# Second experts' first products: 15 block products of thirds for 18, and one plan that orders all engines from there on

## The chip, the cores and the metric

The kernel runs on one core of one Trainium2 chip. The metric is the device time of one execution in microseconds (us); lower is better. TensorE (PE) multiplies, ScalarE (ACT) and VectorE (DVE) read the product banks (PSUM) and work on tiles in SBUF, GpSimd (POOL) works on SBUF tiles, and SyncE (SP) issues the loads and stores.

## What is computed

Attention over 1152 tokens, then a feed-forward layer, then eight experts. Only the experts change here:

```python
def _moe2_ref(x, w_gate, w1, w2):          # x 1152x512, w1 8x512x1024, w2 8x1024x512
    P = np.exp(x @ w_gate - (x @ w_gate).max())
    for _ in range(8):
        P /= P.sum(1, keepdims=True) + 1e-09
        P /= P.sum(0, keepdims=True) + 1e-09
        P *= N / E
    for e in range(E):
        out += P[:, e:e + 1] * (np.maximum(x @ w1[e], 0.0) @ w2[e])
```

Every product is made with operands split in a high and a low part (`hi` is the rounded copy, `lo` the rest), as three matmuls: hi by hi, hi by lo, lo by hi. So one block product over 256 of the 512 input features is 2 x 3 = 6 matmuls.

## The kernel before

**Up to the crossing.** Attention and the start of the feed-forward layer come from a planner (`Plan`, with the table `COST` of busy time and latency by kind of step) that fixes the order of every engine. The end of the feed-forward layer (`gemm1`, `gemm2`, lines 456 and 475) follows in loops. Its result x is formed in four groups of 288 tokens.

**First products of the experts.** The 8 x 1024 hidden features are 64 chunks of 128. Two chunks, two halves of the features of x and two halves of the tokens make a 2 x 2 x 2 problem, which the list `PROD` solves with 7 block products in place of 8 (Winograd's form of Strassen's scheme), a quarter of the tokens (288 columns) at a time. `hidden(h, gp)` (matmuls on line 1192) does this for four chunks h and one of two column positions; two pairs of chunks (`u`) alternate, so that product m of both pairs runs before product m+1 of either. The sums of weights are made by DVE (`e_sums`, line 1077) and split by ACT and POOL (`e_block`, lines 1083 and 1084); the sums of tokens are made once, at the crossing. Partial results are copied out of a bank by ACT (`keep`, line 1179), added by DVE, and rectified and split by ACT and DVE (`done`, lines 1183 and 1184).

**Second products.** `outputs(h, j)` multiplies 128 tokens by the rows of four chunks, 12 matmuls of 512 columns in one bank (line 1230), and DVE adds the bank to `yacc`, with the gate's factor P (line 1241). The rows of w2 are split by ACT and POOL (lines 1104 and 1105). The gate's logits are 40 matmuls of 288 columns (line 1121).

**The crossing** from the feed-forward layer to the experts is written by hand: `first_sums`, `second_sums` and `crossing` (lines 1267 to 1400) interleave the last sums of the feed-forward layer (`inner`, line 1267), the sums of tokens (lines 1275 to 1302) and the first seven products (`product`, line 1315). After it, the tile framework's scheduler chooses the order.

Of the kernel before, what the change touches and what calls it, by code (L numbers as in the profile page):

```python
# [49 lines left out]
    "sum": ("ACT", 0.295, 0.45), "load": ("SP", 0.45, 0.0),  # L50
}
# [10 lines left out]
PORT = {"shift", "sign", "tail", "m", "g", "scale", "fscale", "guard", "vsum", "vsum2", "clamp", "glo", "wlo"}  # L62
# [38 lines left out]
class Step:  # L101
    def __init__(self, **kw):
        self.__dict__.update(kw)
        self.after, self.before, self.left, self.done, self.tail, self.t = [], [], 0, None, 0.0, 0.0


class Plan:
# [34 lines left out]
    def lay(self, tails):  # L142

        rings = {id(z.ring): z.ring for x in self.steps for z in x.b}.values()
        for ring in rings:
            ring.own, ring.k = [None] * len(ring.own), 0
            for z in ring.all:
                z.spot = None
        for x in self.steps:
            x.left, x.done, x.t = len(x.before), None, 0.0  # L150
# [6 lines left out]
        while ready:  # L157
# [20 lines left out]
            if x.eng == "PE" and gap > 0.3:  # L178
# [18 lines left out]
            for y in x.after:  # L197
                y.left -= 1
                y.t = max(y.t, x.done + SEM)
                if not y.left:  # L200
                    ready.append(y)
        if len(log) < len(self.steps):
            return None
        return log

    def back(self, log):
# [3 lines left out]
        behind, ahead, owner = {id(x): list(x.after) for x in self.steps}, {id(x): list(x.before) for x in self.steps}, {}  # L210
# [34 lines left out]
    def run(self):  # L245
# [5 lines left out]
        for n in range(ROUNDS):  # L251
            log = self.lay(tails)
            if not log:
                break
            found.append((self.worth(log), n, log))
            tails = [y + NOISE * rnd.gauss(0.0, 1.0) for y in self.back(log)]
        self.log = min(found)[2]
        for _, x, new, small in self.log:
# [4 lines left out]
            self.emit(x.fn)  # L263
# [3 lines left out]
def attn_moe_moe_kernel(  # L267
# [71 lines left out]
    wg = const.tile([128, KD, NE], F32, name="wg")  # L339

# [27 lines left out]

    def load_w64():
# [13 lines left out]
    def w_raw():  # L383
# [54 lines left out]
    gq, acc, ysum, gl, tx = {}, {}, {}, {}, {}  # L438
# [21 lines left out]
    def gemm2(s):  # L460
# [8 lines left out]
        for d in range(KD):  # L469
# [87 lines left out]
    RE, RMM, RL = (tiles(ap, [128, NMAX], F32, z, 2) for z in ("me", "mm", "ml"))  # L557
# [467 lines left out]
    tx["hi"], tx["lo"] = (tp.tile([128, 3 * KH, NB], F32R, name=f"t{z}") for z in ("hi", "lo"))  # L1025
    for s in range(ATT_END, NS):
# [10 lines left out]
        with tc.issue_after(last["pe"]):  # L1037
# [26 lines left out]

    def e_next(kind, i):
        e_load(order2.index((kind, i)) + ERAW)

    def e_sums(h):

        src = {}  # L1070
        for u in (2 * h, 2 * h + 1):
            r = rw.pop((1, u)).rearrange("p (a b) -> p a b", a=KD)
            s = new(tp, [128, KD * NMAX], F32, "sums", 2)[:, 0:KD * KH * 128].rearrange("p (o a b) -> p o a b", o=4, a=KH)
            w11, w12, w21, w22 = (r[:, k, 128 * f:128 * f + 128] for f in range(2) for k in (first, second))
# [426 lines left out]
```

## Time and profile before

| | |
|---|---|
| runs | 1068.99 us median of 3 (1066.86 to 1069.5) |
| profiled execution, span from first to last instruction | 1065.7 us (the page gives no other time for it) |
| PE busy | 1057.4 us, 99% of the span |
| DVE, ACT, POOL busy | 567.2, 482.8, 338.8 us |
| granted TensorE clock, mean | 0.999 of 2.4 GHz |
| HBM read | 59.93 MB |

A busy time is the union of the times of an engine's instructions. A matmul's row gives its full latency, and the next one starts long before it ends, so a matmul's cost on the path is the distance between starts, not its mean. The rows of DVE, ACT and POOL also overlap a little at their ends.

### The profile page before, as it was taken

Reading aid. Unit: us, or ns where it says so; the run is one execution under the profiler, and the core shown is the slowest. Engines: PE = TensorE matmul, PEld = TensorE weight load, DVE = VectorE, ACT = ScalarE, POOL = GpSimd, SP = SyncE. Lnnn points to the kernel's source line nnn. Section 1 sums busy time; section 2 is a strip of 40 time slices with the busy share of each in tenths; the row PEclk is TensorE's granted clock in tenths of the full one; section 3 lists DMA queues with packets and bytes.
Section 4 is the critical chain, followed back from the end, with each engine's and each line's share of the span. In section 5 each row is a group of like instructions: output and inputs, shape, how many; then the busy total and the mean of one; then the engine's idle time right before and its main releaser. Section 6 shows DMA issues by size and latency. Waiting matters only on the chain.

```text
span 1065.7 us, 19197 instructions
## 1 busy us (share of the span) xinstructions
PE 1057.4 (99%) x7551; PEld 963.6 (90%) x7551; DVE 567.2 (53%) x1225; ACT 482.8 (45%) x1367; POOL 338.8 (32%) x382
## 2 busy tenths in 40 slices
PE   8999999999999999999999999999999999999998
PEld 5899899999998889898898998989999989899997
DVE  6899865452486664545445354444535444444343
ACT  6897875343366434242433424242443424244330
POOL 0343244022047266150513415051432505052300
PEclk9999999999999999999999999999999999999999
DMA  9571322211013020111201111120201111020002
GB/s 220 167 208 38 92 80 79 80 61 40 1 40 99 1 80 31 50 41 40 80 20 60 35 46 40 40 73 9 79 20 60 41 40 47 33 80 21 21 6 84
DMA packets 50179, 63.53 MB, mean 60 GB/s; under 512 B 14888, under 2 KB 33832, under 8 KB 50088
## 3 DMA queue, kind: packets, MB, share of 16 engines
q1 hardware_dynamic: 50088, 62.30, 19.3%
q8 instruction: 59, 0.97, 0.4%
q14 instruction: 32, 0.26, 0.1%
HBM read 59.93 MB, written 2.36 MB: 58 GB/s over the span
## 4 chain that ended last, share of the span: by engine, by line
PE 94%; ACT 2%; DMA 2%; DVE 1%; SPq 1%; issue 0%; POOL 0%; DVEq 0%
PE bank L1230 37%; PE bank L1192 32%; PE bank L456 7%; PE bank L475 7%; PE bank L897 2%; DMA raw<-in_moe_w_in_dram 2%; PE bank L953 2%; PE bank L1315 1%; ACT pl L678 1%; PE bank L611 1%; PE bank L1267 1%; PE bank L738 1%; PE bank L795 1%; PE bank L785 1%; ACT pg L678 1%; PE bank L1121 0%
## 5 line engine op out<-in xcount | busy, mean ns | idle before, releaser
L1230 PE MATMUL bank<-wc,hhi 128*128 128x512 f32 (+1 forms) x1160 | 363.7, 392 | 0.3 <-DVE cs L1154 0.3
L1230 PEld LDWEIGHTS bank<-wc,hhi 128*128 128x128 f32 x1160 | 211.3, 188 | 37.4 <-DVE cs L1154 0.5
L1230 PE MATMUL bank<-wc,hlo 128*128 128x512 f32 x580 | 226.0, 390 | 0.0
L1192 PE MATMUL bank<-xhi,wb 128*128 128x288 f32 x992 | 211.1, 295 | 0.0
L1105 POOL TENSOR_TENSOR wc<-raw,wc 128x512 fp32r<-128x512 f32 x64 | 81.8, 1300 | 341.2 <-ACT wc L1104 341.2
L1192 PEld LDWEIGHTS bank<-xhi,wb 128*128 128x128 f32 x992 | 163.9, 188 | 2.0
L1192 PE MATMUL bank<-thi,wb 128*128 128x288 f32 x744 | 164.6, 295 | 0.0
L1179 ACT ACTIVATE p<-bank 128x288 f32<-128x288 f32 x186 | 76.4, 411 | 173.3 <-PE bank L1192 168.2
L1192 PE MATMUL bank<-xlo,wb 128*128 128x288 f32 x496 | 146.5, 295 | 0.0
L1183 ACT ACTIVATE hhi<-bank 128x288 fp32r<-128x288 f32 x186 | 75.6, 407 | 149.6 <-PE bank L1192 118.3
L1241 DVE SCALAR_TENSOR_TENSOR yacc<-bank,P,yacc 128x512 f32<-128x512 f32 (+1 forms) x127 | 94.5, 744 | 81.2 <-PE bank L1230 81.2
L1184 DVE SCALAR_TENSOR_TENSOR hlo<-bank,hhi 128x288 fp32r<-128x288 f32 x186 | 84.2, 453 | 98.3 <-ACT hhi L1183 94.6
L1230 PEld LDWEIGHTS bank<-wc,hlo 128*128 128x128 f32 x580 | 108.9, 188 | 23.6
L1192 PEld LDWEIGHTS bank<-thi,wb 128*128 128x128 f32 x744 | 124.7, 188 | 3.4
L1084 POOL TENSOR_TENSOR wb<-sums,wb 128x256 fp32r<-128x256 f32 x128 | 93.6, 747 | 76.8 <-ACT wb L1083 74.1
L1192 PE MATMUL bank<-tlo,wb 128*128 128x288 f32 x372 | 109.6, 295 | 0.0
L1084 POOL TENSOR_TENSOR wb<-raw,wb 128x256 fp32r<-128x256 f32 x96 | 72.3, 756 | 83.5 <-PE bank L1192 55.3
L1192 PEld LDWEIGHTS bank<-xlo,wb 128*128 128x128 f32 x496 | 93.3, 188 | 2.6
L1205 DVE TENSOR_TENSOR bank<-bank,p 128x288 f32<-128x288 f32 x62 | 28.7, 463 | 84.9 <-PE bank L1192 82.8
L1192 PEld LDWEIGHTS bank<-tlo,wb 128*128 128x128 f32 x372 | 70.0, 188 | 3.5
L1083 ACT ACTIVATE wb<-sums 128x256 fp32r<-128x256 f32 x128 | 53.1, 417 | 25.8 <-PE bank L1192 23.2
L1198 DVE TENSOR_TENSOR bank<-bank,p 128x288 f32<-128x288 f32 x62 | 28.8, 465 | 54.1 <-ACT p L1179 51.5
(203 smaller groups left out, 1793.2 us busy)
## 6 DMA issues: line engine op xcount, KB each, us to landing
raw<-in_moe_w_dram SPq DMA_DIRECT2D x64, 512.0 KB
raw<-in_moe_w_in_dram SPq DMA_DIRECT2D x16, 512.0 KB
raw<-in_moe_w_out_dram SPq DMA_DIRECT2D x16, 512.0 KB
rawq<-in_q_dram SPq DMA_DIRECT2D x4, 576.0 KB
rawv<-in_v_dram SPq DMA_DIRECT2D x8, 288.0 KB
vw<-in_v_dram SPq DMA_DIRECT2D x12, 192.0 KB
rawq<-in_k_dram SPq DMA_DIRECT2D x3, 576.0 KB
out_dram<-yacc SPq DMA_DIRECT2D x5, 256.0 KB
```

Source lines behind the costliest of these rows:

```text
L456: PE.matmul(out=bk, lhsT=a[:, kk, o], rhs=b[:, kk, c0:c0 + n], start=(i == 0), stop=(i == 3 * KD - 1))
L475: PE.matmul(out=bk, lhsT=a[:, h, o], rhs=b, start=(first and i == 0), stop=(end and i == 2))
L1083: ACT.activation(out=t[:, 0], in_=src[u][w], func=AF.Copy)
L1084: POOL.tensor_tensor(out=t[:, 1], in0=src[u][w], in1=f32(t[:, 0]), op=ALU.subtract)
L1105: POOL.tensor_tensor(out=t[:, 1], in0=r[:, a], in1=f32(t[:, 0]), op=ALU.subtract)
L1179: ACT.activation(out=t, in_=bk[u, b], func=AF.Copy)
L1183: ACT.activation(out=hi, in_=y, func=AF.Relu)
L1184: DVE.scalar_tensor_tensor(out=lo, in0=y, scalar=0.0, in1=f32(hi), op0=ALU.max, op1=ALU.subtract)
L1192: PE.matmul(out=bk[u, b], lhsT=wb[2 * h + u, w][:, wz, kk, :], rhs=ops[xz][:, k + kk, o + c:o + c + NP], start=(m < 3 and i == 0), stop=(i ...
L1198: DVE.tensor_tensor(out=bk[u, "D"], in0=bk[u, "D"], in1=kept[u, "p1"], op=ALU.add)
L1230: PE.matmul(out=bk, lhsT=a[:, f, 128 * j:128 * j + 128], rhs=w[:, b, cs], start=(i == 0), stop=(i == 3 * FH - 1))
L1241: DVE.scalar_tensor_tensor(out=y, in0=bk, scalar=p, in1=y, op0=ALU.mult, op1=ALU.add)
```

## The change

From the crossing on, everything is written anew and ordered by one second plan (`plan2`, 24 passes) over all five engines; nothing is left to the framework's scheduler.

- **Blocks.** Chunk 0 is multiplied directly (36 matmuls of 384 columns). The other 63 chunks are 21 rounds of three. In a round, three chunks, two halves of the features and three thirds of the tokens (384 columns) would be 18 block products; `PROGRAM` makes 15, each of 6 matmuls. It names the bank (A to G) of each product, the copies (`keep`, ACT), the sums (`add`, `sum`, DVE) and the nine results (`out`).
- **Sums of tokens.** Twelve (`XSUMS`) in place of three. Each is 768 elements wide: formed by DVE (`form`), its high part copied by ACT (`formhi`), its low part made by POOL for eight of them (`formlo2`) and by DVE for four (`formlo`). They read `xs0` and `xs1`, two new tiles with x in full precision. When the last of them has read these, the tiles' memory becomes two buffers for rows of w2 (`late0`) and the six buffers of kept copies (`keeps`), so no `keep` can start sooner.
- **Sums of weights.** Eleven of 256 elements in a round (`wsum`, DVE) and 15 splits (`wh` on ACT, `wl` on POOL).
- **Second products** have three chunks in a bank (9 matmuls of 512 columns), and are added to `yacc` after each round; where a round spans two experts, twice. There are three buffers of split rows for the three chunks of a round, and one of each hidden block.
- **Logits** are 24 matmuls of 384 columns for 40 of 288.
- **Loads** are 768 KB of w1 for a round (one transfer or two) and 256 KB of w2 for a chunk, for 512 KB each before.
- In the part before the crossing the order is the same but for a few matmuls of the last chunks; some tiles are slices of one larger tile now.

```diff
+PORT = {"shift", "sign", "tail", "m", "g", "scale", "fscale", "guard", "vsum", "vsum2", "clamp", "glo", "wlo", "wsum", "form", "formlo"}
+WPLAIN = {2: 0, 9: 3, 10: 5, 14: 4}
+WSUMS = [(0, "b2", 1, "b3", -1), (3, "b2", 1, "b4", 1), (5, "b1", 1, "b3", 1), (7, "b3", -1, "f3", 1),
...
+XPLAIN = {0: 1, 4: 3, 6: 2}
+XSUMS = [(9, "b1", -1, "b4", -1), (7, "b1", -1, "b3", 1), (10, "f7", -1, "f9", 1), (3, "b0", 1, "b3", 1),
...
+XHOME = {8: "m", 5: "b0", 12: "b4", 2: "b5"}
+XTEMP = {9: "m0", 7: "r", 10: "m1", 3: "t0", 14: "t1", 5: "r", 11: "t0", 13: "t1", 1: "t2", 8: "r", 12: "t0", 2: "t2"}
+XEARLY = {9, 7, 10}
+XPOOL = {9, 7, 10, 3, 14, 8, 12, 2}
+PASSES2 = 24
+WHEN = [(1, 8), (1, 2), (2, 0), (2, 10), (2, 3), (2, 1), (2, 11), (2, 5)]
+
+PROGRAM = """
+prod 9 A new; keep p A; prod 0 B new; keep q B; sum p p - q +; out 4 p; prod 14 C new; keep r C; prod 10 D new; keep s D
+prod 7 B; keep t B; prod 3 C; add C - t; out 3 C; prod 4 B; keep u B; add B - r; out 6 B; sum s s - u -; out 7 s; prod 1 D
+prod 13 A; keep v A; prod 11 E new; keep w E; add D - w; keep x D; prod 8 C; add C - v; prod 5 A; keep y A; add A + w
+out 1 A; prod 6 F new; add F - x; out 8 F; prod 12 D; out 2 D; add D - y; prod 2 G new; keep z G; add D + z; out 0 D
+add C + z; out 5 C
+"""
+MOST2 = {"acc": 4, "g1": 6, "g2": 2, "g2x": 8}
...
+        c0 = groups[g][0] * TQ
+        return [xs[d // KH][:, d % KH, c0:c0 + NMAX] for d in range(KD)]
...
+    TH = NT // 3
+    xform = tp.tile([128, 8, 2, KH, TH], F32R, name="xform")
+    xs = [new(tp, [128, KH, NT], F32, f"xs{k}", 1) for k in range(2)]
+    wop0 = tp.tile([128, 2, KH, 128], F32R, name="wop0")
...
-    PROD = [(W12, 0, KH, 0, "D"), (W11, 0, 0, 0, "A"), (S1, 0, 0, NB, "C"), (S2, 1, 0, 0, "A"), (S4, 0, KH, NB, "C"),
-            (S3, 1, KH, 0, "A"), (W22, 1, 2 * KH, 0, "A")]
...
-    def hidden(h, gp):
...
-    def outputs(h, j, cs=slice(0, DM)):
...
-    pin(first_sums)
...
-    pin(crossing)
...
-    for h in range(NH):
-        if h:
-            hidden(h, 0)
-            for j in range(5, NTL):
-                outputs(h - 1, j)
-            e_rows(2 * h + 1)
-        hidden(h, 1)
-        e_blocks(h + 1)
-        for j in range(5):
-            outputs(h, j)
-        e_rows(2 * h + 2)
-    for j in range(5, NTL - 1):
...
+    NC = NE * NFE
+    rounds_ = [[0]] + [list(range(i, i + 3)) for i in range(1, NC, 3)]
...
+    RW, RC, R2 = Ring(8, wplace), Ring(3, cplace), Ring(4, r2place)
+    RK = Ring(6, lambda i: m["keeps"][:, TH * i:TH * i + TH], {"k": 6})
...
+    def p_sum_(n, p, ca, q_, cb):
+        ftemp[n] = Buf(FR[XTEMP[n]])
+        add("form", lambda n=n, p=p, ca=ca, q_=q_, cb=cb: signed(DVE, ftemp[n].t, term(p), ca, term(q_), cb),
+            r=fkeys(p) + fkeys(q_) + fextra(n), w=[("xf", n)], b=fbufs(n, p, q_))
+    def p_split_(n):
+        h = homes[n]
+        own = [("pb", int(h[1:]))] if isinstance(h, str) and h != "m" else []
+        add("formhi", lambda n=n: ACT.activation(out=operand(n)[0], in_=ftemp[n].t, func=AF.Copy),
+            r=[("xf", n)] + fextra(n) + (["ap"] if h == "m" else []), w=[("xfh", n)] + own, b=fbufs(n))
+        add("formlo2" if n in XPOOL else "formlo", lambda n=n, eng=eng: eng.tensor_tensor(
+            out=operand(n)[1], in0=ftemp[n].t, in1=f32(operand(n)[0]), op=ALU.subtract),
+            r=[("xf", n), ("xfh", n)] + fextra(n), w=[("xfl", n)], b=fbufs(n))
...
+    def late_():
+        m["late0"] = new(tp, [128, KH * NT], F32R, "xs0", 1)
+        m["keeps"] = new(tp, [128, KH * NT], F32, "xs1", 1)
...
+    add("open", late_, r=["ap"], w=["xs", "late"])
...
+    def p_products(r, wop, hb):
...
+                def pe(n=n, y=y, bb=bb, fresh=fresh):
+                    x, i = operand(n), 0
+                    for kk in range(KH):
+                        for wz, xz in ((0, 0), (0, 1), (1, 0)):
+                            PE.matmul(out=bb.t[:, 0:TH], lhsT=y.t[:, wz, kk, :], rhs=x[xz][:, kk, :], start=(fresh and i == 0),
+                                      stop=(i == 3 * KH - 1), skip_group_check=True)
+                            i += 1
...
+            elif op[0] == "keep":
+                kb[op[1]] = y = Buf(RK, "k")
+                src, key = where(op[2])
+                add("keep", lambda src=src, y=y: ACT.activation(out=y.t, in_=src.t[:, 0:TH], func=AF.Copy), r=[key, "late"],
+                    w=[("b", id(y))], b=[src, y])
+            elif op[0] == "add":
+                (z, key), (y, yk) = where(op[1]), where(op[3])
+                add("add", lambda z=z, y=y, c=SIGN[op[2]]: signed(DVE, ap_(z), ap_(z), 1, ap_(y), c), r=[yk], w=[key], b=[z, y])
...
+    def p_outputs(r, cs, hb, wc):
...
+                                for i, (hz, wz) in enumerate(((0, 0), (0, 1), (1, 0))):
+                                    PE.matmul(out=bk.t[:, a:b], lhsT=h[hz][:, js], rhs=y[:, wz, a:b],
+                                              start=(f == fs[0] and i == 0), stop=(f == fs[-1] and i == 2))
...
+        wop = p_weights(r, cs)
+        wc = p_rows(r, cs)
+        hb = {(f, t): Buf(RH[f, t]) for f in range(3) for t in range(3)}
+        p_products(r, wop, hb)
+        p_outputs(r, cs, hb, wc)
+    plan2.run(PASSES2)
```

Three places where the order moved:

DVE at the crossing, before the change (`t`: sums of tokens, `xlo` and `tlo`: low parts, `ysum` and `wb`: parts of x, `bank`: products):

```order
L1297 TENSOR_TENSOR xlo<-wb_2462,xhi 128x288
L1297 TENSOR_TENSOR tlo<-t_3934,thi 128x288
L1297 TENSOR_TENSOR tlo<-t_3936,thi 128x288
L1302 TENSOR_TENSOR t_3982<-t_3934,ysum 128x288
L1302 TENSOR_TENSOR t_3986<-ysum,t_3934 128x288
L1275 TENSOR_TENSOR bank_112<-bank_112,wb_2886 128x288
L1275 TENSOR_TENSOR bank_117<-bank_117,wb_2887 128x288
L1278 TENSOR_TENSOR wb_2886<-bank_112,ysum 128x288
L1278 TENSOR_TENSOR wb_2887<-bank_117,ysum 128x288
```

And with the change, the stretch up to the last sum that reads `xs1` (here `xs_2291`; `temp` and `raws` hold sums of tokens, `xform` and `xlo` their low parts, `P` and `mx` belong to the gate, `hlo` to chunk 0):

```order
L1249 TENSOR_TENSOR wsums<-raws,wsums 128x256 x2
L1249 TENSOR_TENSOR wsums<-raws 128x256
L1399 COPY P<-bank_115 128x72
L1400 TENSOR_TENSOR P<-bank_115,P 128x72
L1402 TENSOR_REDUCE mx<-P 128x1
L1326 SCALAR_TENSOR_TENSOR hlo<-bank_119,hhi 128x384
L1314 MEMSET ones 128x128
L1249 TENSOR_TENSOR temp<-xs_2290,temp 128x768
L1289 TENSOR_TENSOR xform<-temp,xform 128x768
L1249 TENSOR_TENSOR temp<-xs_2290,temp 128x768
L1289 TENSOR_TENSOR xlo<-raws,xhi 128x2x384
L1249 TENSOR_TENSOR temp<-xs_2290,xs_2291 128x768
```

The last row is the sum for product 12. From the first sum of tokens to it DVE now has 10 sums of 768 elements, 4 low parts of x of 576, 7 sums of weights of 256 and 2 low parts of 768, all with two SBUF operands; before, this work was 288 wide and stood among sums that read a bank.

PE around the first product that adds to a bank already used, with the change (line 1505: products of `PROGRAM`; 1405: the gate's maximum; 1553: second products of chunk 0):

```order
L1505 MATMUL bank_116<-xform,wops 128x384 x6
L1405 MATMUL bank_115<-ident,mx 128x128
L1553 MATMUL bank_119<-wc_3903,hhi 128x512 x2
L1553 MATMUL bank_119<-wc_3903,hlo 128x512
L1505 MATMUL bank_113<-xform,wop_2292 128x384 x6
L1505 MATMUL bank_118<-xform,ysum 128x384 x6
L1553 MATMUL bank_115<-wc_3903,hhi 128x512 x2
```

The first row is product 10, the fifth product 7. Product 7 adds to bank B (here `bank_113`), which holds product 0, so it needs the copy of product 0 (`keep q`) done. Before, the place was taken by products of 288 columns for two pairs of chunks and sums of the feed-forward layer:

```order
L1267 MATMUL bank_117<-ghi,lo_3432 128x288
L1315 MATMUL bank_116<-xhi,wb_3885 128x288
L1315 MATMUL bank_116<-xlo,wb_3885 128x288
L1315 MATMUL bank_116<-xhi,wb_3885 128x288 x2
L1315 MATMUL bank_116<-xlo,wb_3885 128x288
L1315 MATMUL bank_116<-xhi,wb_3885 128x288
L1267 MATMUL bank_118<-ghi,hi_3367 128x288
```

PE in the second round, products 7, 3 and 4 (between them one matmul of the gate):

```order
L1505 MATMUL bank_119<-xform,wops 128x384 x6
L1505 MATMUL bank_117<-xform,wop_2292 128x384 x6
L1437 MATMUL bank_113<-P,ones 128x72
L1505 MATMUL bank_119<-xhi,ysum 128x384
L1505 MATMUL bank_119<-xlo,ysum 128x384
```

Products 7 and 4 share bank B (here `bank_119`) with only product 3 between them, and `keep t` has to copy the bank in that time; `hidden` had three products of 288 columns between two uses of a bank.

## Rows read from the trace of the kernel before

**Rows 1.** The page: busy time of the engines, and the chain that ended last.

```profile
PE 1057.4 (99%) x7551; PEld 963.6 (90%) x7551; DVE 567.2 (53%) x1225; ACT 482.8 (45%) x1367; POOL 338.8 (32%) x382
...
PE 94%; ACT 2%; DMA 2%; DVE 1%; SPq 1%; issue 0%; POOL 0%; DVEq 0%
```

**Rows 2.** Stretches: crossing to the last matmul, the gate, one steady group.

```profile
core 0: us, PE busy (x) PEld busy (x) DVE busy (x) ACT busy (x) POOL busy (x), PEclk, DMA share, GB/s
290.40:1062.84 772.44, 771.90 (x4556) 698.40 (x4554) 378.99 (x817) 297.76 (x767) 262.39 (x299) 1.00 0.14 45
...
340.00:400.00 60.00, 59.46 (x351) 53.42 (x350) 37.85 (x121) 23.75 (x58) 23.87 (x23) 1.00 0.13 45
...
473.16:520.28 47.12, 47.12 (x277) 42.58 (x277) 22.03 (x45) 17.79 (x48) 15.26 (x19) 1.00 0.13 45
```

**Rows 3.** The chain in steady work: start, us, engine, line, matmuls.

```profile
473.16 4.13 PE bank L1230 x18
...
507.90 4.80 PE bank L1192 x36
```

**Rows 4.** Order of time at the end, PE and DVE: start, us.

```profile
1059.31 0.51 PE L1230 MATMUL bank<-wc,hhi 128*128 128x384 f32 x2
...
1061.39 0.33 PE L1230 MATMUL bank<-wc,hhi 128*128 128x128 f32 x2
...
1062.56 0.28 PE L1230 MATMUL bank<-wc,hlo 128*128 128x128 f32 x1
1062.88 0.35 DVE L1241 SCALAR_TENSOR_TENSOR yacc<-bank,P,yacc 128x128 f32<-128x128 f32 x1 [0.67 <-PE bank L1230]
```

**Rows 5.** Order of time of DVE at the crossing.

```profile
291.00 0.87 DVE L1275 TENSOR_TENSOR bank<-bank,wb 128x288 f32<-128x288 f32 x2 [1.03 <-PE bank L1267]
...
297.08 0.99 DVE L1302 TENSOR_TENSOR t<-t,ysum 128x288 f32<-128x288 f32 x1
297.99 0.99 DVE L1302 TENSOR_TENSOR t<-ysum,t 128x288 f32<-128x288 f32 x1
...
300.37 0.44 DVE L1302 TENSOR_TENSOR t<-t,ysum 128x288 f32<-128x288 f32 x1
300.74 0.45 DVE L1302 TENSOR_TENSOR t<-ysum,t 128x288 f32<-128x288 f32 x1
...
327.66 1.41 DVE L1184 SCALAR_TENSOR_TENSOR hlo<-p,hhi 128x288 fp32r<-128x288 f32 x1
```

**Rows 6.** Order of time of POOL at the crossing.

```profile
297.72 0.95 POOL L1084 TENSOR_TENSOR wb<-raw,wb 128x256 fp32r<-128x256 f32 x1
298.63 1.79 POOL L1297 TENSOR_TENSOR tlo<-t,thi 128x288 fp32r<-128x288 f32 x2
...
303.30 1.44 POOL L1084 TENSOR_TENSOR wb<-sums,wb 128x256 fp32r<-128x256 f32 x2 [0.37 <-ACT wb L1083]
...
323.46 5.29 POOL L1105 TENSOR_TENSOR wc<-raw,wc 128x512 fp32r<-128x512 f32 x4
```

**Rows 7.** Groups by line and shape: busy us, mean ns of one, idle before.

```profile
L1241 DVE SCALAR_TENSOR_TENSOR yacc<-bank,P,yacc 128x512 f32<-128x512 f32 x125 | 93.5, 748 | 79.2 <-PE bank L1230 79.2
...
L1077 DVE TENSOR_TENSOR sums<-raw 128x256 f32<-128x256 f32 x64 | 26.0, 445 | 38.4 <-DMA raw<-in_moe_w_dram 37.3 <-POOL yacc L1239 0.8
...
L854 DVE SCALAR_TENSOR_TENSOR raw<-raw,raw 128x512 uint32<-128x512 uint32 x16 | 10.9, 681 | 0.1
...
L801 DVE TENSOR_TENSOR bank<-bank,odT 128x384 f32<-128x384 f32 x12 | 6.7, 559 | 0.8 <-ACT odT L745 0.6 <-PE bank L795 0.2
...
L810 ACT ACTIVATE xhi<-bank 128x384 fp32r<-128x384 f32 x12 | 5.9, 495 | 0.6 <-DVE bank L801 0.6
...
L1084 POOL TENSOR_TENSOR wb<-sums,wb 128x256 fp32r<-128x256 f32 x128 | 93.6, 747 | 76.8 <-ACT wb L1083 74.1 <-issue 1.8
L1105 POOL TENSOR_TENSOR wc<-raw,wc 128x512 fp32r<-128x512 f32 x64 | 81.8, 1300 | 341.2 <-ACT wc L1104 341.2
```

**Rows 8.** The stretch after the last matmul, columns as in rows 2.

```profile
1063.00:1066.00 3.00, 0.00 (x0) 0.00 (x0) 0.23 (x1) 0.00 (x0) 0.00 (x0) 0.70 0.25 87
```

More of the change, by code (lines that the diff above doesn't have):

```diff
@@ L201, in lay @@
                     ready.append(y)
+            for y in x.next:
+                y.left -= 1
+                if not y.left:
+                    ready.append(y)
         if len(log) < len(self.steps):
@@ L209, in back @@
         begin = {id(x): t for t, x, _, _ in log}
-        behind, ahead, owner = {id(x): list(x.after) for x in self.steps}, {id(x): list(x.before) for x in self.steps}, {}
+        behind, ahead, owner = {id(x): x.after + x.next for x in self.steps}, {id(x): x.before + x.prev for x in self.steps}, {}
         for _, x, new, _ in log:
@@ L243, in worth, with follow, run @@
         return ends[0] + OTHER * max(0.0, ends[1] - ends[0] - SLACK)
-    def run(self):
+    def follow(self, x, y):
+        if x is not None:
+            x.next.append(y)
+            y.prev.append(x)
+        return y
+    def run(self, rounds=ROUNDS):
         tails = {}
@@ L250, in run @@
         rnd, found = random.Random(SEED), []
-        for n in range(ROUNDS):
+        for n in range(rounds):
             log = self.lay(tails)
[L253 to L257, printed above, removed]
+            if log:
+                found.append((self.worth(log), n, log))
+                late = self.back(log)
+            tails = [y + NOISE * (1 if log else 5) * rnd.gauss(0.0, 1.0) for y in late]
+        self.log = min(found, key=lambda f: f[:2])[2]
         for _, x, new, small in self.log:
@@ L1068, in e_sums @@
[L1068 to L1074, printed above, removed]
-            for o, a, b, op in ((0, w21, w22, ALU.add), (1, s[:, 0], w11, ALU.subtract), (2, w11, w21, ALU.subtract),
-                                (3, w12, s[:, 1], ALU.subtract)):
-                DVE.tensor_tensor(out=s[:, o], in0=a, in1=b, op=op)
-            src[u] = {W11: w11, W12: w12, W22: w22, S1: s[:, 0], S2: s[:, 1], S3: s[:, 2], S4: s[:, 3]}
-        return src
@@ L1293, in upper @@
-    def upper(y, hi, lo):
-        ACT.activation(out=hi, in_=y, func=AF.Copy)
-    def lower(eng, y, hi, lo):
-        eng.tensor_tensor(out=lo, in0=y, in1=f32(hi), op=ALU.subtract)
-    def other(g, m, k):
-        moved[g, k, m] = v = new(tp, [128, NMAX], F32, f"t{m + 2}", 1)
-        t, x = moved[g, k], ysum[g - 2][k if m == 1 else KH + k]
-        DVE.tensor_tensor(out=v, in0=t if m == 1 else x, in1=x if m == 1 else t, op=ALU.subtract)
-        upper(*tparts(g, m, k))
-        lower(POOL, *tparts(g, m, k))
@@ new lines, in attn_moe_moe_kernel, with lgp @@
+    add("lgt", lgt, r=[("lg", t) for t in range(3)], w=[("b", id(bk)), "lgt"], b=[bk])
+    def lgp(bk=bk):
+        P, flatp = gate_steps()
+        b4 = bk.t[:, 0:2 * NE * NTL].rearrange("p (j t e) -> p j t e", t=2, e=NE)
+        DVE.tensor_copy(out=P, in_=b4[:, :, 0, :])
+        DVE.tensor_tensor(out=P, in0=b4[:, :, 1, :], in1=P, op=ALU.add)
+        st["mx"] = tp.tile([128, 1], F32, name="mx")
+        DVE.tensor_reduce(out=st["mx"], in_=flatp, axis=AX.X, op=ALU.max)
+    add("lgp", lgp, r=[("b", id(bk)), "ap"], w=["P"], b=[bk])
@@ new lines, in attn_moe_moe_kernel @@
+    steps_ = []
+    for _ in range(8):
+        bk = bank2()
+        steps_.append(add("row", row, w=["P"]))
+        add("one", lambda bk=bk: PE.matmul(out=bk.t[:, 0:NTL * NE], lhsT=m["ones"], rhs=gate_steps()[1], start=True, stop=True),
+            r=["P", "ones"], w=[("b", id(bk))], b=[bk])
+        add("col", partial(col, bk), r=[("b", id(bk))], w=["P"], b=[bk])
+    wsrc = {n: (p, ca, q_, cb) for n, p, ca, q_, cb in WSUMS}
+    program = [x.split() for line in PROGRAM.replace("\n", ";").split(";") for x in [line.strip()] if x]
```

745 lines of the change are left out of this document (390 added, 355 removed).

## The prediction

> **What bounds the kernel now.** Read the page's busy times first, then its chain: PE is busy for 1057.4 us, 99% of the span, and 94% of the chain that ended last is PE [rows 1]. The table of stretches says the same of the part that changes. From the first sum of the crossing (290.40) to the end of the last matmul (1062.84) PE is busy for 771.90 of 772.44 us, all at a granted clock of 1.00, the upper of its two levels (2.4 GHz); the 0.54 us of idle time lie where the gate waits [rows 2]. One group of four chunks takes 47.12 us without a gap, while DVE, ACT and POOL have 22, 18 and 15 us of work [rows 2]. So a matmul removed is worth its distance to the next, as long as the other engines keep PE fed.
>
> **The distances.** 18 matmuls of 512 columns take 4.13 us in the chain, 229.4 ns each [rows 3]. A group is 168 matmuls of 288 columns and 108 of 512, so the 288 ones are (47.12 - 108 x 0.2294) / 168 = 133.0 ns apart [rows 2, 3]; 36 in 4.80 us (133.3) agree [rows 3]. The last tile has 12 matmuls of 384 columns, from 1059.31 to 1061.39: 173.3 ns each [rows 4]. That is the price of the new products. A straight line between 288 and 512 would give 174.3, scaling by columns alone 177.3; this is the bound upwards.
>
> **What goes and comes on PE.** Away: 16 groups x 168 = 2688 matmuls of first products and 40 of the logits, 2728 x 0.1330 = 362.8 us. New: 21 rounds x 90 + 36 = 1926 matmuls of 384 columns and 24 of the logits, 1950 x 0.1733 = 337.9 us. PE saves 24.9 us; at 177.3 ns it would be 17.1. The second products keep their columns (1719 matmuls of 512 for 1716, the split tile as before): 0. The 60 matmuls of the last feed-forward sums stay. A round is 15.6 us of first and 18.6 of second products, 34.2 in all.
>
> **The crossing** is the part that may give time back. PE reaches product 7 after 60 x 0.133 + 60 x 0.1733 (logits and chunk 0) + 24 x 0.1733 + 3 x 0.2294 + 0.7 for the gate's small ones (an estimate) = 24 us. Product 7 adds to bank B and waits for `keep q`, which waits until the last sum that reads xs1 is made, as those buffers lie in its memory. Up to there DVE has 23 instructions with two SBUF operands. A 288-wide one takes a step of 0.37 us when POOL is quiet (300.37 to 300.74) [rows 5]. From 288 to 512 elements the duration grows from 0.44 to 0.681 us [rows 5, 7], 1.08 ns an element, so I take 0.89 us for 768, 0.68 for 576 and 0.34 for 256: 12 x 0.89 + 4 x 0.68 + 7 x 0.34 = 15.8 us. Eight sums from banks and six short ones at 0.37 or less add 5.2, two waits for ACT's copy of x some 1.5, and the first starts 0.6 after the crossing [rows 5]: 23 us. Alone, DVE is in time, and nothing waits: that is the lower end, 0.
>
> But POOL works beside it. At 297.08 and 297.99 the same 288-wide sums last 0.99 us and are 0.91 apart while POOL makes low parts, and one that stands beside POOL's 512-wide splits lasts 1.41 us for 0.44 [rows 5, 6]. POOL slows less: 256 elements go from 0.72 (two in 1.44) to 0.95 us [rows 6]. By then POOL has 5 low parts of 768 elements, 10 splits of 256 and one of 512. At 0.72 and 1.30 us [rows 6, 7] a further 256 elements cost 0.58, so 768 cost 1.88 and the sum is 9.4 + 7.2 + 1.3 = 17.9 us. If DVE stood still for all of it, the gate would open at 41 us and PE would lose 17: the upper end. The nearest row is the pair at 297: 0.54 us lost for each POOL instruction of about 0.9, some 60%. About 12 of the 17.9 us fall beside two-operand work (23 us hold 15.8 of it), so DVE loses 7 us and the gate opens at 30: PE idles 6 us before product 7, and I add 1 for the logits of the last third of tokens, which need DVE's last low part of x. So 7 us of idle PE.
>
> The Trainium skill ("SBUF — State Buffer", section "SBUF: two separate sides") calls the pair of ports that VectorE and GpSimd share an exclusive lock, held for the whole instruction, which fully blocks the other. By that rule the 12 us would count in full, and the sum would be 5 us longer; the row with 1.41 us speaks for it, the pair at 297 for a little less.
>
> **Rounds.** In a round DVE has 11 sums of weights at 0.445, 20 sums and low parts at 0.559 and 9 additions at 0.748 us: 22.8 of 34.2 us, and 29.5 in the five rounds that span two experts. POOL has 15 x 0.747 + 3 x 1.30 = 15.1 [rows 7]. Both are covered by PE. What the averages don't show is the fixed order: `keep t` has the 1.04 us of product 3 to copy bank B, and takes 0.495 [rows 7], so an ACT instruction of the same length ahead of it just fits. I take 1 us for all rounds; the ends are 0 and 1 us a round, 20.
>
> Transfers cost nothing: 1.57 MB in 34.2 us are 46 GB/s, for 45 now at a DMA share of 0.13 [rows 2]. They wait longer for buffers (one pair for w1, three for w2's split rows), but the next round's rows are wanted 15 us after the old ones are free; without that cover a round would wait for its 3 x 1.30 us of splits. The end stays: 2.9 us from the last matmul through the last addition to the last store [rows 4].
>
> **Sum.** 1065.7 - 24.9 + 7 + 1 = 1048.8 us of span. The median of the runs is 3.3 above the profiled span, so I expect **1052 us**.
>
> **Rivals.**
> (a) The cover holds: much of POOL's work waits for sums that DVE has yet to make, so they collide less. Against it: sums of weights and their splits come in the same stretch. The crossing costs 0 to 3 us and the time is 1044 to 1048.
> (b) Each collision costs the whole POOL instruction: by the 12 us that meet, 5 us more, 1057. Then PE would stand still for most of 10 us, and in the 3 us after the last matmul of this trace the clock's mean is 0.70, so its lower level (1.2 GHz) had set in [rows 8]. If it did here, 4 to 8 us of products at half speed would add 4 to 8 us at most: 1057 to 1064. For it: the 1.41 us.
> (c) The fixed order loses a little in every round. `keep t` behind one copy and one split, or a bank of the second products not emptied, costs 0.3 to 0.7 us a round: 1058 to 1066.
> (d) The same, dearer: product 4 regularly waits for `keep t`. From 0.8 us a round the 20 later rounds eat what is left (16.9), and with 1.0 us, about one more product, it is slower than before: 1071. Against it: ACT has less than 20 us of work in a round of 34.
> (e) That the columns are not saved is ruled out by the order, which lists 1890 matmuls of 384 columns for the rounds. Only their price could be off, by up to 7.8 us (177.3 ns), against 12 matmuls in a row; this is inside the others' ranges.
>
> **Chances.** Forecast 0.45 (its own range 1048 to 1057), (a) 0.20, (b) 0.17, (c) 0.11, (d) 0.07. A measurement of this kernel tells about 0.3% (3.2 us) from no change. Faster by more, below 1065.8: forecast, (a), (b) and most of (c), 0.91. Within: 0.04. Slower: most of (d), 0.05. The range 1045 to 1063 leaves out the low end of (a), some of (c) and (d), together 0.2.
>
> **What would show it.** A round of 34.2 us without a gap, and 384-wide matmuls 173 ns apart, show the saving; a longer round with PE idle before line 1505 shows (c) or (d), and the name of the releaser which: ACT's `keep` on line 1519 or the second products' bank. At the crossing, PE idle before product 7 until ACT's copy, itself behind DVE's 768-wide sums, shows the forecast's loss; those sums at 0.9 us mean (a), near 2 us (b). A clock below 1.00 just after is (b)'s second part. The forecast is wrong if rounds are not PE's, or if PE waits at the crossing for something else, such as w1's second transfer.

## The result and the profile after

The change made the kernel slower. The median of the runs is 1079.2 us beside 1068.8 us for the kernel before, a ratio of 1.010 with a 95% interval of 1.0085 to 1.012. The forecast was 1052 us, its range 1045 to 1063.

The page of the changed kernel, busy times and the first line of its chain, to be read beside [rows 1]:

```profile
PE 1051.3 (98%) x6770; PEld 948.5 (88%) x6770; DVE 783.2 (73%) x1394; ACT 538.0 (50%) x1429; POOL 445.6 (41%) x474
...
PE 83%; DVE 11%; ACT 3%; DMA 2%; issue 1%; POOL 0%; SPq 0%; DVEq 0%; ACTq 0%
```

PE is busy for 6 us less than before, where 24.9 were to be saved, and 11% of the chain is now DVE's. The span is 1077.7 us; the forecast's sum was 1048.8, so 28.9 us have to be found. The table of stretches, columns as in [rows 2], splits the part that changed in two: from the first sum of the crossing to 460 us, and from there to the last matmul.

```profile
290.50:460.00 169.50, 152.94 (x753) 136.84 (x752) 147.10 (x269) 80.91 (x184) 99.12 (x92) 0.94 0.16 47
460.00:1074.60 614.60, 613.25 (x3023) 546.60 (x3022) 451.58 (x726) 273.31 (x651) 273.95 (x305) 1.00 0.14 44
```

In the first 169.5 us PE is idle for 16.6 us, and its clock is granted at 0.94 in the mean. Afterwards it is idle for 1.35 us in 614.6. Three things show in these two rows.

**Waits at the crossing.** The order of time of PE; the bracket is the idle time ahead of an instruction and who ended it:

```profile
295.64 0.61 PE L1195 MATMUL bank<-ghi,hi 128*128 128x288 f32 x1 [2.52 <-DVE glo L499]
...
324.38 2.29 PE L1505 MATMUL bank<-xform,wop 128*128 128x384 f32 x6 [3.68 <-ACT xs L1519]
...
351.78 0.67 PE L1437 MATMUL bank<-P,ones 128*128 128x72 f32 x2 [4.81 <-ACT xs L1519]
```

The middle row is product 7 waiting for `keep`, as the forecast had it. The first is a wait of the old feed-forward layer's last sums. The third is a product of the gate that waits for a bank. Neither stood in the forecast. The order of time of DVE tells why PE waits in the first two:

```profile
292.74 0.95 DVE L1251 TENSOR_TENSOR raws<-xs,xs 128x768 f32<-128x768 f32 x1
293.61 0.95 DVE L1253 SCALAR_TENSOR_TENSOR mt<-xs,xs 128x768 f32<-128x768 f32 x1
294.47 0.75 DVE L1214 TENSOR_TENSOR xlo<-xs,xhi 128x576 fp32r<-128x576 f32 x1
295.14 0.45 DVE L499 TENSOR_TENSOR glo<-bank,ghi 128x288 fp32r<-128x288 f32 x1
295.51 2.24 DVE L1251 TENSOR_TENSOR mt<-mt,raws 128x768 f32<-128x768 f32 x1
297.68 2.39 DVE L1214 TENSOR_TENSOR xlo<-xs,xhi 128x576 fp32r<-128x576 f32 x1
...
322.57 0.95 DVE L1249 TENSOR_TENSOR temp<-xs,xs 128x768 f32<-128x768 f32 x1
```

and of POOL:

```profile
294.64 2.30 POOL L1289 TENSOR_TENSOR xform<-raws,xform 128x768 fp32r<-128x768 f32 x1 [11.41 <-ACT xform L1286]
296.90 4.88 POOL L1289 TENSOR_TENSOR xform<-mt,xform 128x768 fp32r<-128x768 f32 x2
```

`glo`, which PE needs at 293, stands behind two sums and a low part of x. The sum at 295.51 takes 2.24 us, where the same shape took 0.95 two rows earlier: POOL's low part runs until 296.94 (294.64 + 2.30), and DVE's sum ends 0.81 us behind that, as if it had only begun there. The last sum that reads xs1 starts at 322.57; `keep` is free at 323.4, 33 us after the crossing began. PE itself comes to product 7 at 320.70 (324.38 - 3.68), 30 us after the crossing began.

The third wait ends with a copy on ACT:

```profile
350.33 0.72 ACT L1478 ACTIVATE ysum<-wsums 128x256 fp32r<-128x256 f32 x2 [3.06 <-DVE wsums L1249]
...
351.26 0.47 ACT L1519 ACTIVATE xs<-bank 128x384 f32<-128x384 f32 x1
```

The copy that empties the bank stands in ACT's fixed order behind splits of weights, and for these ACT itself waits 3.06 us for a sum that DVE makes behind steps of the gate.

**A lower clock.** The granted clock (the last column but two) in four stretches. Each begins in or just after a wait of PE, of 2.52, 3.68, 4.81 and, ahead of 441.58, 2.13 us:

```profile
295.40:298.80 3.40, 3.15 (x13) 3.16 (x14) 3.40 (x3) 0.88 (x2) 3.40 (x2) 0.50 0.00 0
322.70:329.50 6.80, 5.12 (x15) 4.92 (x16) 6.80 (x10) 6.24 (x15) 4.79 (x5) 0.50 0.00 0
350.00:356.80 6.80, 5.02 (x16) 5.05 (x17) 6.12 (x21) 2.65 (x7) 2.11 (x3) 0.50 0.14 42
442.10:445.50 3.40, 3.40 (x9) 2.63 (x9) 2.64 (x6) 0.00 (x0) 3.40 (x3) 0.51 0.00 0
```

For 20.4 us TensorE ran at the lower of its two levels, 1.2 GHz. PE's order of time shows what that costs:

```profile
296.05 0.44 PE L1195 MATMUL bank<-glo,hi 128*128 128x288 f32 x1
296.29 0.44 PE L1195 MATMUL bank<-ghi,lo 128*128 128x288 f32 x1
```

The 288-wide matmuls are 240 ns apart there, for 133.0 at the upper level: 1.8 times as far. At that factor the 16.7 us of work in the four stretches would have taken 9.1, so about 7.6 us are lost (an estimate).

**Wider spacing in rounds that have no gap.** The chain in steady work, beside [rows 3]:

```profile
564.30 14.70 PE bank L1505 x84
579.00 16.76 PE bank L1553 x72
595.76 1.04 PE bank L1505 x6
596.80 2.10 PE bank L1553 x9
598.90 14.71 PE bank L1505 x84
```

A round takes 34.60 us, for 34.2 forecast. The 384-wide matmuls are 175.0 ns apart (14.70 / 84) for 173.3 forecast, and the 512-wide ones 232.8 (16.76 / 72) for 229.4, though not one of these matmuls waits. Over 1950 and 1719 matmuls that is 3.3 + 5.8 = 9.1 us.

The sum: 16.6 us of idle time, 7.6 of clock and 9.1 of spacing, with 1.35 after 460 us, less the 8 us that the forecast held, make 26.7 of the 28.9 us; 2.2 us stay open. The idle time is a lower bound, since the modelled end of the matmul ahead of a wait counts as work.

### The profile page after: what moved, and what is told of

Same layout as the page of the kernel before. It is cut to its first block, busy times and chain, and to the rows that moved or that the text cites. A ratio compares the mean times of both kernels' runs of the same rounds, so it can differ in the third digit from the quotient of the medians.

```text
span 1077.7 us, 18231 instructions
## 1 busy us (share of the span) xinstructions
PE 1051.3 (98%) x6770; PEld 948.5 (88%) x6770; DVE 783.2 (73%) x1394; ACT 538.0 (50%) x1429; POOL 445.6 (41%) x474
## 4 chain that ended last, share of the span: by engine, by line
PE 83%; DVE 11%; ACT 3%; DMA 2%; issue 1%; POOL 0%; SPq 0%; DVEq 0%; ACTq 0%
PE bank L1553 35%; PE bank L1505 25%; PE bank L511 7%; PE bank L530 7%; DVE wsums L1249 3%; PE bank L946 2%; PE bank L1002 2%; DMA raw<-in_moe_w_in_dram 1%; PE bank L660 1%; ACT pl L727 1%; DVE bank L1249 1%; DVE hlo L1326 1%; DMA rawq<-in_q_dram 1%; PE bank L787 1%; PE bank L844 1%
## 5 line engine op out<-in xcount | busy, mean ns | idle before, releaser
L1566 DVE SCALAR_TENSOR_TENSOR yacc<-bank,P,yacc 128x512 f32<-128x512 f32 x208 | 152.8, 745 | 138.9 <-PE bank L1553 138.2
L1553 PE MATMUL bank<-xs,hhi 128*128 128x512 f32 (+1 forms) x760 | 239.6, 396 | 3.4 <-DVE yacc L1564 2.1
L1553 PEld LDWEIGHTS bank<-xs,hhi 128*128 128x128 f32 x760 | 142.4, 189 | 35.0 <-DVE yacc L1564 2.6
L1519 ACT ACTIVATE xs<-bank 128x384 f32<-128x384 f32 x231 | 112.7, 489 | 116.3 <-PE bank L1505 72.4
L1553 PE MATMUL bank<-xs,hlo 128*128 128x512 f32 (+1 forms) x380 | 150.3, 396 | 0.0
L1553 PE MATMUL bank<-wc,hhi 128*128 128x512 f32 (+1 forms) x398 | 124.9, 395 | 0.0
L1249 DVE TENSOR_TENSOR bank<-bank,xs 128x384 f32<-128x384 f32 x189 | 101.1, 557 | 20.5 <-ACT xs L1519 16.9
L1505 PE MATMUL bank<-xform,wops 128*128 128x384 f32 x564 | 109.5, 340 | 1.1 <-POOL wops L1480 1.1
L1249 DVE TENSOR_TENSOR wsums<-raws 128x256 f32<-128x256 f32 x147 | 106.1, 743 | 1.4 <-POOL wops L1480 1.4
L1553 PEld LDWEIGHTS bank<-wc,hhi 128*128 128x128 f32 x398 | 74.4, 188 | 16.4
```

The costliest lines, as they stand in the source:

```text
L1249: eng.tensor_tensor(out=out, in0=a, in1=b, op=ALU.add if cb > 0 else ALU.subtract)
L1505: PE.matmul(out=bb.t[:, 0:TH], lhsT=y.t[:, wz, kk, :], rhs=x[xz][:, kk, :], start=(fresh and i == 0), stop=(i == 3 * KH - 1), skip_group_c ...
L1519: add("keep", lambda src=src, y=y: ACT.activation(out=y.t, in_=src.t[:, 0:TH], func=AF.Copy), r=[key, "late"], w=[("b", id(y))], b=[src, y])
L1553: PE.matmul(out=bk.t[:, a:b], lhsT=h[hz][:, js], rhs=y[:, wz, a:b], start=(f == fs[0] and i == 0), stop=(f == fs[-1] and i == 2))
L1566: DVE.scalar_tensor_tensor(out=y, in0=bk.t[:, a:b], scalar=p, in1=y, op0=ALU.mult, op1=ALU.add)
```

## The experiments

Two questions: what makes PE wait at the crossing, and what widens the spacing. For the first, **theory L** says that DVE and POOL shut each other out and that together they have more work due in the first round than PE's work can cover. Its rivals name one place that all waits for: the memory of xs1 and ACT's order (**G**), or the gate's eight steps (**S**). What L stands for moved in the course: in e1, e2 and e4 it is the shutting out, in e5 and p1 the sum of work, and in e3 the sum of work stands under G. For the second, **theory A** says that TensorE gives a fixed number of columns per us, **theory P** that it depends on where the operands lie, and B and Q are their opposites. "Before" was run beside each group, with medians of 1068.0 to 1068.3 us.

### Spacing: narrower matmuls

```diff
# c1_288: in rounds from the second on, all of a first product's instructions
+        NW = TH if r < 2 else 288
...
-PE.matmul(out=bb.t[:, 0:TH], lhsT=y.t[:, wz, kk, :], rhs=x[xz][:, kk, :], ...
+PE.matmul(out=bb.t[:, 0:NW], lhsT=y.t[:, wz, kk, :], rhs=x[xz][:, kk, 0:NW], ...
# c2_256
-for a, b in ((0, 384), (384, 512)) if end and j == LAST else ((0, DM),):
+for a, b in ((0, 384), (384, 512)) if end and j == LAST else ((0, 256),) if 1 < r < 21 else ((0, DM),):
```

> The changed kernel with first products that are 288 columns wide from the second round of three blocks on: a quarter of the tokens' columns is left out there, and the sums, copies and low parts of them too. The order of instructions is the same. Theory A (in the steady part TensorE gives a fixed number of columns per us, 2200: the old group's 103680 columns in 47.12 us and the new round's 76032 in 34.60 us both give that): 90 x 288 + 81 x 512 = 67392 columns take 30.6 us, and the 512-wide matmuls go back to about 230.4 ns apart. Rival B (each matmul has its own price in this kernel, raised by operands' places or busier neighbours): the 512-wide ones stay at 232.7 ns or more, and a round takes 30.8 us.

> The changed kernel with second products of 256 columns in place of 512 from the second round of three blocks to the last but one: half of the output's columns is left out there. The order of instructions is the same. Theory A: the narrow matmuls run below the fixed rate, so the 384-wide ones go back from 175 to 173.3 ns apart, and a round takes about 25.3 us if VectorE keeps up. Rival B: the 384-wide ones stay at 175 ns.

The chain of the first, and then of the second:

```profile
628.14 16.77 PE bank L1554 x72
...
647.80 11.17 PE bank L1506 x84
```

```profile
568.67 4.19 PE bank L1505 x24
573.55 2.10 PE bank L1505 x12
```

Beside 288-wide matmuls, 133.0 ns apart, the 512-wide ones stay at 232.9 ns; beside 256-wide ones the 384-wide ones stay at 174.6 to 175.0. **Theory A fell**, though both kernels' columns per us had agreed with it: a matmul's price here does not depend on its neighbours' width. (The two, with one execution each, took 1026.2 and 916.1 us; DVE no longer kept up in places.)

### The crossing: the planner's list, and POOL's work

```diff
# e1_list
-PORT = {..., "glo", "wlo", "wsum", "form", "formlo"}
+PORT = {..., "glo", "wlo", "wsum", "form", "formlo", "formlo2", "pairlo", "wl"}
# e2_lows: the same, and
-XPOOL = {9, 7, 10, 3, 14, 8, 12, 2}
+XPOOL = set()
```

> The changed kernel with one line altered: the planner's list of work that may not run side by side on VectorE and GpSimd now also holds GpSimd's splits of weights, GpSimd's low parts of x's sums and VectorE's low parts of x; nothing is computed differently, only the order differs. Theory L (the two engines shut each other out, and the plan did not know it): the plan then puts the waits where they cost least, the 27 us that TensorE loses between 290 and 460 us fall to about 15, and the time is 1067 us (1063 to 1071). Rival G (the loss is the copy that waits for xs1's memory and ScalarE's fixed order, whatever the list says): the loss stays, 1076 to 1082 us. Rounds keep 34.6 us under both.

> As the run with the longer list, and all 12 low parts of x's sums are made on VectorE (8 of them were GpSimd's). VectorE gets 8 x 0.87 = 7 us more work at the crossing; GpSimd loses 8 instructions of 1.9 to 2.4 us, 15 to 17 us. Theory L: VectorE stood still for those, so it gains 8 to 10 us net, the loss between 290 and 460 us falls from 27 to about 9 us, and the time is 1061 us (1057 to 1066). Rival G: VectorE's queue is 7 us longer, the gate opens later, and the time is 1080 to 1087 us.

e1 took 1070.5 us (ratio to before 1.0023, 1.0012 to 1.0034): 8.7 us of the 10.4 came back by the order alone. That is inside L's range and fits a plan that had been made with false durations. Of the 8.7 us 3.3 are idle time, and most of the rest is the clock, by the table below. (The plan is the best of 24 passes with random numbers in them, so some of the 8.7 may be another draw; no run tells.) e2 took 1067.9 us (1.0001, 0.9991 to 1.0012), above L's 1066 and far below G's 1080, so that both missed. The lock's part was right: in e2's order of time of DVE the sum that took 2.24 us takes 0.95 again.

```profile
296.34 0.45 DVE L499 TENSOR_TENSOR glo<-bank,ghi 128x288 fp32r<-128x288 f32 x1
296.71 0.95 DVE L1251 TENSOR_TENSOR mt<-mt,raws 128x768 f32<-128x768 f32 x1
297.57 0.75 DVE L1214 TENSOR_TENSOR xlo<-xs,xhi 128x576 fp32r<-128x576 f32 x1
```

But `glo` still stands behind two sums and a low part, and new waits had come, by the list of PE's waits from 285 to 470 us:

```profile
PE bank L1437 <- DVE P L1421: 3.8, 4, 1.8
PE bank L1195 <- DVE glo L499: 2.5, 1, 2.5
PE bank L1505 <- ACT ysum L1478: 1.2, 1, 1.2
PE bank L1505 <- ACT xs L1519: 0.9, 2, 0.7
```

### The crossing: one wait, or the sum of work?

```diff
# e3_order: e2, and
+    pinned[mybir.EngineType.Activation] = last["mish"].ins.name
...
+    add("glo2", last["glo"], r=["ghi", "ap"], w=["glo"])
# e4_gate: the changed kernel; e5_both: e3; with
-WHEN = [(1, 8), (1, 2), (2, 0), (2, 10), (2, 3), (2, 1), (2, 11), (2, 5)]
+WHEN = [(2, 8), (2, 2), (3, 0), (3, 10), (3, 3), (3, 1), (3, 11), (3, 5)]
...
-            tails = [y + NOISE * (1 if log else 5) * rnd.gauss(0.0, 1.0) for y in late]
+            tails = [y + NOISE * (1 if log else 5) * rnd.gauss(0.0, 1.0) for y in (late if found else tails)]
```

> As the run with all low parts of x's sums on VectorE, and one thing more: the last low part of the old layer (glo, line 499) and the copy before it now have their place in the plan, ahead of the sums of x; until now the plan did not know that instruction, and it stood behind two 768-wide sums and a low part, while TensorE waited 2.5 us and its clock then showed the lower level for 3.4 us. Theory L and the order: TensorE's wait of 2.5 us ahead of line 1195 and the low clock after it go, 2.5 + 1.7 = about 4 us, 1064 us (1062 to 1066). Rival G (the crossing is bound further back, by VectorE's sum of work, so what is won early is waited for later): 1066 to 1069 us.

> The changed kernel with one line altered: the gate's eight steps start a round later, so that they leave the first round of three blocks (where the first pass of the planner finds no order it may go on from its starting values). Theory S (the gate's steps, which wait on VectorE behind sums and stand in TensorE's fixed order, make the second half of the loss): TensorE's waits ahead of line 1437 in 340 to 375 us (4.8 + 1.3 + 1.3 us) and the low clock after 350 us go, the time falls by 6 to 10 us to 1069 to 1073. Theory L (the engines' shutting out is what counts, the gate only stands where the queue is late): another instruction waits in its place, 1074 to 1080 us.

> The run with all low parts of x on VectorE and the old layer's last low part in the plan, with the gate's eight steps a round later. Theory S: the 5.0 us ahead of the gate's products and the low clock of 3.4 us after them go, 1066.3 - 7 = 1059 us (1057 to 1062). Theory L: the first round's sums, splits and low parts fill VectorE by themselves, products wait in place of the gate, 1063 to 1068 us.

e3 took 1066.3 us (0.9986, 0.9976 to 0.9996), just above L's range and inside its rival's: the wait for `glo` shrank from 2.5 to 0.2 us, but of the 4 us expected only 1.6 came, and the gate's line waited 5.0 us for 3.8. The copies that G names end only 1.9 of e3's 9.0 us of idle time:

```profile
PE bank L1511 <- ACT xs L1525: 1.9, 3, 0.9
```

e4 took 1075.4 us (1.0066, 1.005 to 1.0083) and e5 1066.2 us (0.9981, 0.997 to 0.9993), both in L's range and outside S's. PE's waits in e5 show what happens when the gate is taken away:

```profile
PE bank L1511 <- ACT xs L1525: 2.9, 3, 1.4
PE bank L1511 <- DVE xform L1295: 1.3, 1, 1.3
PE bank L1511 <- POOL wops L1486: 1.2, 2, 1.0
PE bank L1443 <- DVE P L1427: 1.2, 1, 1.2
PE bank L1559 <- DVE yacc L1570: 1.0, 1, 1.0
```

In e3 the gate's line had held 5.0 us, and now it holds 1.2. Copies, a low part of x, splits of weights and additions hold PE in small pieces instead. Single waits change place. That fits a bound by all the work due, and S falls.

### The crossing: less work due

```diff
# p1_plain: e3, and for the first round of three blocks
-        p_products(r, wop, hb)
+        if r == 1:
+            wc, hb = p_rows(r, cs), hb1
...
+    for t in range(3):
+        for f in range(3):
+            for k in range(2):
+                x = add("direct", pe, ...
...
-WHEN = [(1, 8), (1, 2), (2, 0), (2, 10), (2, 3), (2, 1), (2, 11), (2, 5)]
+WHEN = [(2, 9), (2, 10), (2, 7), (2, 4), (2, 13), (2, 8), (2, 5), (2, 2)]
```

With it, `late` is split into one key for each half of xs, three of the sums' temporaries lie in the memory of the sums of weights, and the gate's rows and columns and the short sums stand in the planner's list. In this kernel and in c3 and c4 below, the sum of x for product 2 takes one operand from memory in which a row of weights may lie by then, so that sum is another one; the instructions are the same in kind and number. p4 makes it in time.

> As the run before it, and the first round of three blocks is made by 18 plain products (x as it is, no sums) in place of 15: 18 matmuls of 384 columns more, 3.15 us, and in return the 12 sums of x are wanted a round later, the first round needs 6 splits of weights for 15 and no sums of weights, keeps and second products' rows wait each for its own half of x's memory alone, and the gate's eight steps start a round later. Theory L (VectorE's and GpSimd's work within 45 us is too much for the time that TensorE can give it): TensorE's idle time between 290 and 460 us falls to 3 to 5 us, and the time is 1058 us (1055 to 1062). Rival G: the same waits for memory and for ScalarE come a round later, and with the 3 us added the time is 1066 to 1072 us.

> As the run with 18 plain products in the first round, with the twelfth sum of x (product 2's operand) made before the next rows of weights may take its memory, and the gate's first two steps already in the first round. Theory L: the crossing stays nearly without waits, and the time is 1055 us (1053 to 1058). Rival G: the sum that now has to come earlier holds up the rows of the second products, TensorE waits 5 us or more before them, 1060 us or more.

p1 took 1055.1 us (0.9876, 0.9861 to 0.989), p4 1055.6 us (0.9885, 0.9872 to 0.9899), both in L's range and below G's. The row of p4 that answers to the first stretch above:

```profile
290.50:460.00 169.50, 169.12 (x884) 153.72 (x883) 138.62 (x286) 85.08 (x191) 85.32 (x90) 1.00 0.18 55
```

PE idles for 0.4 us, at a clock of 1.00 throughout. The runs on the crossing and p5 side by side, by this row:

| run | time, us | PE idle in 169.5 us | mean granted clock |
|---|---|---|---|
| changed kernel | 1079.2 | 16.6 | 0.94 |
| e4 gate later | 1075.4 | 14.3 | 0.96 |
| e1 longer list | 1070.5 | 13.3 | 0.98 |
| e2 no low parts on POOL | 1067.9 | 10.3 | 0.98 |
| e3 `glo` in the plan | 1066.3 | 9.0 | 0.98 |
| e5 e3, gate later | 1066.2 | 10.1 | 1.00 |
| p1 first round plain | 1055.1 | 1.2 | 1.00 |
| p4 p1, product 2's sum in time | 1055.6 | 0.4 | 1.00 |
| p5 p4, operands moved (below) | 1052.0 | 0.3 | 1.00 |

The times are medians, the other columns are of one trace. e2's trace is of its longest execution, 1071.3 us.

p4 closes the account: 1068.0 - 24.9 saved + 9.1 of spacing + 3.2 for its extra matmuls (18 x 0.175) gives 1055.4 us.

So the loss at the crossing goes when less is due in the first round. Which part of it counts is not shown: p1 takes away sums, splits and kept copies of the first round at once, gives the twelve sums of x a round more time, splits the wait for the memory of xs in two and moves the gate's steps. POOL's splits of weights stayed in every run, so the shutting out was never taken away alone either.

### Spacing: where operands lie

```diff
# c3_hlo: p1, and
+        mp.tile([128, 128], F32, name="gap")
         m["hlo"] = mp.tile([128, 3, NT], F32R, name="hlo")
# c4_xs: p1; p5_place: p4; with (in c4 the tile is named tpad)
+        DVE.memset(tp.tile([128, 160], F32, name="gap"), 0.0)
```

> As the run with 18 plain products in the first round, with 512 bytes left free ahead of hlo, so that hhi and hlo lie at the same place within 2048 bytes again, as in the kernel before, and all that follows lies 512 bytes on. Nothing else changes. Theory P (the spacing of 232.7 ns, for 229.9 in the kernel before, comes from where the operands lie): the 512-wide matmuls move by 1 ns or more. Rival Q (it comes from elsewhere): 232.7 and 175.0 to 175.2 stay within 0.3 ns.

> As the run with 18 plain products in the first round, with 640 bytes left free behind xs, so that xform and the memory of xs, in which two of three rows of second weights lie, start 640 bytes earlier. Nothing else changes. Theory P (the spacing comes from where the operands lie): the 512-wide or the 384-wide matmuls move by 1 ns or more. Rival Q: 232.7 and 175.0 to 175.2 stay within 0.3 ns.

> As the run before it in this call, with xform and the memory of xs 640 bytes earlier. Theory P (where operands lie sets 1 to 2 ns of each matmul): 1719 x 1.5 ns + 1977 x 0.4 ns = 3.4 us less, 1052 us (1050 to 1054), with 512-wide matmuls 231.0 ns apart for 232.5. Rival Q (the difference between the two earlier runs was chance): the same time within 1 us.

The chains of p1, c3 and c4, 48 second products in a row in each, and for p1 and c4 54 others a little later:

```profile
592.27 11.20 PE bank L1598 x48
...
625.74 12.57 PE bank L1598 x54
```

```profile
592.55 11.20 PE bank L1600 x48
```

```profile
591.85 10.99 PE bank L1599 x48
...
625.11 12.51 PE bank L1599 x54
```

512 bytes ahead of `hlo` change nothing: 233.3 ns in both, as rival Q had it. 640 bytes at xs change these 48 to 229.0, but the 54 only from 232.8 to 231.7. (c3 and c4, with one execution each, took 1056.0 and 1053.2 us.) p4 and p5 repeat it, for first and second products:

```profile
582.97 7.37 PE bank L1550 x42
590.34 8.40 PE bank L1598 x36
```

```profile
583.07 7.32 PE bank L1551 x42
590.39 8.24 PE bank L1599 x36
```

Here 233.3 ns go to 228.9, and 175.5 to 174.3; other stretches move less. All pieces of the chain from 465 to 1040 us together give 232.6 and 230.8 ns for second products, and 175.3 and 175.0 for first ones. At those means 1719 and 1968 matmuls take 3.7 us less. p5 took 1052.0 us beside p4's 1055.6: 3.6 us less, for 3.4 expected. **Theory P holds** for xs and `xform`, not for `hlo`. p5 is the best version: ratio to before 0.985 (0.9837 to 0.9864). Its account closes too: its means are 1.4 and 1.7 ns above the forecast's prices, 5.7 us in all, and 1068.0 - 24.9 + 3.2 + 5.7 gives 1052.0.

## Why the prediction was wrong

Of the 28.9 us the crossing took the most: 16.6 of idle time and 7.6 of clock, for 7 forecast. The distances took 9.1, for 0.

**The distances were mis-sized by 9.1 us.** "The second products keep their columns", with a change of 0, priced 1719 matmuls by [rows 3] of another kernel, 229.4 ns, and they measured 232.8; the first products measured 175.0 for 173.3, a price from 12 matmuls. Case (e) bounded only the first products. The step that failed carried a price over from one kernel to another. Runs c4 and p5 show that the place of operands is one reason: moving xs and `xform` gave back 3.6 us, 1.8 ns in the mean of the second products. Where the 5.7 us that p5 still has come from is open.

**The crossing: the mechanism was right, its extent was not.** Product 7 did wait for `keep q`, the gate opened after 33 us for 30 forecast, and three 768-wide sums took 2.2 to 2.6 us beside POOL. PE waited there only 3.68 us for 6 forecast, by luck: earlier waits and the lower clock behind the first of them had made PE itself late, 30 us for 24. The exclusive lock that the Trainium skill describes ("SBUF — State Buffer", section "SBUF: two separate sides") agrees with the traces: the sum at 295.51 ended 0.81 us after POOL's instruction, about its own length. The forecast's 60% for such meetings was too low. (POOL had even less to do by then than forecast: 5 splits of 256 elements by 323, for 10.) Yet e2 took POOL's low parts out of these meetings, with the longer list of e1, and the two together won only 11 us of the 27 needed for 1052. The failed step is "So 7 us of idle PE": it added up DVE's work only as far as `keep q` and let PE run free behind it. What was due behind that (further sums, 15 splits, 11 sums of weights, the gate's eight steps; the gate was priced at 0.7 us of PE alone) kept DVE nearly full. The changed kernel and then p4:

```profile
290.50:360.00 69.50, 56.45 (x294) 53.05 (x293) 63.00 (x103) 41.02 (x88) 43.13 (x35) 0.88 0.15 47
```

```profile
290.50:360.00 69.50, 69.25 (x397) 65.65 (x396) 58.98 (x131) 41.13 (x84) 26.28 (x29) 1.00 0.22 65
```

DVE was busy for 63.0 of the first 69.5 us, in which 13.1 of the 16.6 us of idle time lie, and PE stood in smaller pieces up to 460. (DVE's busy time alone is not the measure: e3 has 64.9 us of it and 8.0 of idle PE.) Also `glo`, which the plan did not know, cost 2.5 us before the first product. e3, e4 and e5 show that neither `glo` nor the gate's steps were the cause by themselves; p4 shows that the loss goes when less is due in the first round.

**The clock** was rival (b)'s second part: 20.4 us at the lower level and about 7.6 us lost, where (b) had 4 to 8. But (b) priced it for the wait at product 7 alone, and it came behind four waits.

**What held.** The columns were saved: p4's and p5's accounts close with the 24.9 us. Rounds have no gap, so (c) and (d) fell: `keep t` costs nothing, and 1.35 us of idle time in 614.6 answer to the 1 us forecast. Transfers cost nothing: no wait of PE from 285 us on names one. From the start of the last matmul (1074.25) to the span's end are 3.4 us, for 2.9 forecast from its end.

**The chances.** Slower had 0.05, all of it for a wait in every round. That the crossing alone could eat 24.9 us was left out, though its upper end, 17 us, with (b)'s clock and case (e)'s price already came to it: the bounds had been taken one at a time.

## What to carry to other kernels

When a change makes a stage's other engines busy, add up all the work due up to the next point where PE runs free, not only up to the first wait, and count work of DVE and POOL that reads two SBUF operands as one queue. A planner that lays out such a stage must hold every instruction of that queue in its list, or its order is wrong where it is tightest; and here 3 us more of PE work, with 12 sums moved a round later, won 11. A spacing read in a few rows of one kernel is not yet the price in the next.

## What was not expected of the hardware

The distance between matmuls that wait for nothing depends on where their operands lie in SBUF: 640 bytes moved 512-wide matmuls from 232.6 to 230.8 ns in the mean, and from 233.3 to 228.9 in one stretch of a round, while 512 bytes at another operand did nothing. The 384-wide ones moved by 0.3 ns in the mean. What about the place counts was not tried. Columns per us, equal in both kernels (103680 in 47.12 us, 76032 in 34.60, 2200 each), were a coincidence that c1 and c2 took apart.
